# Where group 3's k is scaled: VectorE behind its q, or GpSimd behind the w_in loads

## The chip, the cores and the metric

The kernel runs on one core of a Trainium2 chip. The metric is the device time in microseconds (us). A core has five engines with instruction queues of their own: TensorE (PE in the profile, with its weight loads as PEld), VectorE (DVE), ScalarE (ACT), GpSimd (POOL) and SyncE (SP, which here only issues DMAs). Each engine runs its queue in order; engines wait for each other through semaphores.

## The reference

Attention with normalised q and k for 8 batches and 12 heads (448 rows, 64 columns each), then a feed-forward block whose input is the attention's output with the heads side by side:

```python
q_n = q / sqrt(mean(q * q, -1) + 1e-6) * g_q          # k_n in the same way, with g_k
scores = q_n @ k_n.T / 8
attn = softmax(scores)
x = (attn @ v), heads side by side                    # 3584 x 768
h = x @ w_in                                          # 768 x 2048
g = max(h, 0) + alpha * min(h, 0)
out = g @ w_out                                       # 2048 x 768, float32
```

## The kernel before

The 96 heads are worked on in 24 groups of four heads, three groups to a batch. A group's q and k go through the same steps:

- load_qk(y) issues the loads of q and k on SP, in natural order (128 partitions x 896 numbers each, float32). Four buffers named nat take turns; groups 2, 5 and 8 use places in a large tile called arena instead. A buffer is loaded again once the scale step of its former group has read it: q of group 6 goes where q of group 3 was, k of group 6 where k of group 3 was.
- square (line 376, on POOL) squares them, reduce (line 395, DVE) sums each row, and root (lines 416 and 417, ACT) makes the reciprocal root, rr.
- scale(y, q) and scale(y, k) (line 436) multiply by rr and write fp16. Groups 1, 3 and 5 write to places in the arena, one for q and one for k, so group 3 writes over group 1; other groups write to tiles named qs. The engine of this multiply is chosen in the code.
- turn(y) (lines 560 to 569) turns both with seven PE transposes each (q first) into two PSUM banks and copies them out on DVE into qT and kT. From group 9 on another layout without PE transposes is used (line 423 is its scale).
- score, soft: PE makes scores (line 588) and ACT takes the exponential (line 602), for each of 7 blocks j. den (PE, line 613), log and invert (ACT, lines 666 and 671) make the reciprocal sums; attend (PE, line 613) multiplies by v; times (DVE, line 709) scales the result into xT. Two groups of a batch share one den, log, invert and attend, "0+1"; the third has its own.

The feed-forward block follows batch by batch: begin and up (PE, line 726) multiply xT by w_in, slope (ACT, line 766) and larger (DVE, line 772) make g, and down and its successors multiply by w_out. begin(0) to begin(3) do the first two thirds of a product, those of groups 0 and 1, before group 2's xT is there; up(0,0) is the first that needs times(2,0,0).

The weights come through DMAs that POOL issues: load_w_in(c) has four issues of line 339 for each quarter c, and four more of line 347 where c is 0 or 2; load_w_out (line 353) and load_v (line 329) are issued there too. The issues of w_in wait for earlier ones to land when too many are under way. spin steps are PE work with no use but to keep PE busy.

follow(y, nm) (line 507) is a copy on POOL of one column of a scaled tile into a tile called mark; it makes POOL's queue follow what DVE wrote.

The order of all this is written out by hand: PLAN is a string of steps, read from front to back, and each step puts its instructions at the end of the queues of the engines that it uses. A step's place in the string thus sets its place in each queue, and nothing else. Around the change the string has root(3), invert(0+1), scale(3,q), score(2,2,0), load_w_in(3), two soft steps, two times steps, scale(3,k), square(4,q), times(0+1,0,0), turn(3).

Of the kernel before, what the change touches and what calls it, by code (L numbers as in the profile page):

```python
# [35 lines left out]
soft(1,2) score(0,5,1) score(1,1,0) soft(0,5) soft(1,1) score(1,5,0) turn(2) soft(1,5) score(1,6,1)  # L36
soft(1,6) reduce(3,q,None) score(1,4,0) score(2,0,0) soft(1,4) den(0+1,0) follow(1,k) soft(2,0)
log(0+1) load_qk(5) score(2,1,0) spin(1) reduce(3,k,0+1) attend(0+1,1,0) score(2,6,0) score(2,4,1)
attend(0+1,0,1) soft(2,1) root(3) score(2,3,1) invert(0+1) scale(3,q) score(2,2,0) load_w_in(3)
soft(2,4) soft(2,6) times(0+1,1,0) times(0+1,1,1) scale(3,k) square(4,q) times(0+1,0,0) turn(3)  # L40
score(2,5,0) square(4,k) load_qk(6) reduce(4,q,None) soft(2,3) soft(2,2) soft(2,5) den(2,0) log(2)
reduce(4,k,None) invert(2) attend(2,0,1) score(3,0,1) square(5,q) square(5,k) times(2,0,0)
score(3,1,0) begin(0) reduce(5,q) square(6,q) soft(3,0) begin(1) up(0,0,0) load_w_out(0) reduce(5,k)
# [150 lines left out]
def kernel(  # L194
# [12 lines left out]
    nc = tc.nc  # L207
# [7 lines left out]
    G = HH // 2  # L215
# [119 lines left out]
    def load_w_in(c):  # L335

        src = moe_w_in[:512].rearrange("(n x p) f -> n p x f", n=4, p=32)
        for n in range(4):
            nc.gpsimd.dma_start(
                out=w_in_sb[ds(32 * n, 32), :4, ts(c, FB)], in_=src[n, :, :, ts(c, FB)]  # L340
            )
        if c % 2 == 0:
            w = ts(c // 2, 2 * FB)
            src = moe_w_in[512:].rearrange("(n g e p) f -> e n p g f", n=2, g=2, e=2)
            for e in range(2):
                for n in range(2):
                    nc.gpsimd.dma_start(
                        out=w_in_sb[ds(64 * e + 32 * n, 32), 4:, w], in_=src[e, n, :, :, w]
                    )
# [11 lines left out]
    def square(y, nm):  # L361
        if y >= TD:
            t = nat[y, nm]
            sqs[y, nm] = t[:, :, HD:]
            nc.gpsimd.tensor_mul(out=sqs[y, nm], in0=t[:, :, :HD], in1=t[:, :, :HD])  # L365
            return
        src = nat[y, nm].rearrange("p h j d -> p (h j d)")
        sqf = sqs[y, nm].rearrange("p n d -> p (n d)")
        if (y, nm) == (1, "q"):
            nc.scalar.activation(out=sqf, in_=src, func=AF.Square)  # L370
        else:

            n = 2 if (y, nm) in ((2, "q"), (G, "k")) else 1
            for h in range(n):
                c = ts(h, 2 * J * D // n)
                nc.gpsimd.tensor_mul(out=sqf[:, c], in0=src[:, c], in1=src[:, c])
# [31 lines left out]
    def root(y, nms="qk"):  # L408
        n = len(nms)
        at = "qk".index(nms[0])  # L410
        if at == 0:
            rr_t[y] = ld.tile([128, 2, 2, 2, J], FP32, name="rr", tag="rr", bufs=2)
            if y < TD:
                rr_t[y] = rr_t[y][:, 0]
        rr, ss = rr_t[y][:, ds(at, n)], ss_t[y][:, ds(at, n)]
        nc.scalar.activation(out=rr, in_=ss, func=AF.Ln, scale=1.0 / D, bias=RMS_EPS)
        nc.scalar.activation(out=rr, in_=rr, func=AF.Exp, scale=-0.5)  # L417

    def scale(y, nm):
        if y >= TD:  # L420
            t = ld.tile([128, J, HD, 4], FP16, name="qs", tag="qs", bufs=3)
            r = rr_t[y][:, "qk".index(nm)].rearrange("p g h j -> p (g h) j")
            nc.gpsimd.tensor_mul(  # L423
                out=t.rearrange("p j d n -> p n j d"),
                in0=nat[y, nm][:, :, :HD].rearrange("p (n j) d -> p n j d", j=J),
                in1=r.unsqueeze(3).broadcast_to((128, 4, J, HD)),
            )
            qs[y, nm] = t.rearrange("p j d n -> p (j d n)").bitcast(FP32)
            return
        if y in (1, 3, 5):  # L430
            t = lent(HB + 4 * NB4 + "qk".index(nm) * NB4 // 2, NB4 // 2).bitcast(FP16)
            t = t.rearrange("p (j h d) -> p j h d", j=J, h=2)
        else:
            t = ld.tile([128, J, 2, D], FP16, name="qs", tag="qs", bufs=3)
        eng = nc.vector if y < G or (y, nm) == (G, "q") else nc.gpsimd
        eng.tensor_mul(
            out=t.rearrange("p j h d -> p h j d"),
            in0=nat[y, nm],
            in1=rr_t[y][:, "qk".index(nm)].unsqueeze(3).broadcast_to((128, 2, J, D)),
        )  # L440
        qs[y, nm] = t
# [101 lines left out]
    def turn(y):  # L543

        if y >= TD:
            for nm in "qk":
                if (y, nm) not in qkT:
                    flip(y, nm)
            return
        if y <= G or y > 2 * G:  # L550
            ps = [psf.tile([128, 512], FP32, name="tps", tag="mm") for _ in "qk"]
        else:
            ps2 = psa.tile([128, 2, 512], FP32, name="tps2", tag="acc")
            ps = [ps2[:, 0], ps2[:, 1]]
        tps = [
            t[:, : S].bitcast(FP16).rearrange("p (j c) -> p j c", j=J) for t in ps
        ]
        for tp, nm in zip(tps, "qk"):
            for j in range(J):
                nc.tensor.transpose(  # L560
                    tp[:, j, :], qs[y, nm][:, j].rearrange("p h d -> p (h d)"), ident
                )
        for tp, nm in zip(tps, "qk"):
            t = att.tile([128, J, 2, 64], FP16, name=f"{nm}T", tag=f"{nm}T", bufs=2)
            o = t.rearrange("p j g c -> p j (g c)")
            if nm == "q":
                nc.vector.tensor_copy(out=o, in_=tp)
            else:
                nc.vector.tensor_scalar(
                    out=o, in0=tp, scalar1=gain[:, 0:1], scalar2=None, op0=ALU.mult  # L570
                )
            qkT[y, nm] = t
# [7 lines left out]
    def score(y, j, spare=False):  # L580
        qT, kT = qkT[y, "q"], qkT[y, "k"]
        pool, tag = (psa, "acc") if spare else (pss, "sc")
        sc = pool.tile([128, 2, 512], FP32, name="sc", tag=tag)
        m = 64 if y < EARLY else 32
        for c in range(64 // m):
            for par in range(2):
                for g in range(2):
                    nc.tensor.matmul(  # L588
                        out=sc[ds(64 * g + m * c, m), par, :S].rearrange(
                            "p (j c) -> p j c", j=J  # L590
                        ),
                        lhsT=kT[ds(64 * par, 64), j, g, ts(c, m)],
                        rhs=qT[ds(64 * par, 64), :, g, :],
                        start=True,
                        stop=True,
                    )
        scs[y, j] = sc

    def soft(y, j):
        if j == 0:  # L600
            expT[y] = att.tile([128, J, 2, S], FP16, name="expT", tag="expT", bufs=EB)
        nc.scalar.activation(  # L602
            out=expT[y][:, j], in_=scs[y, j][:, :, :S], func=AF.Exp,
            scale=QK_SCALE, bias=EXP_BIAS,
        )
# [63 lines left out]
    def invert(ys):  # L669
        r = rden[ys]  # L670
        nc.scalar.activation(out=r, in_=r, func=AF.Exp, scale=-1.0)  # L671
# [3 lines left out]
    def attend(ys, half, spare=False):  # L675

        b, i = divmod(ys[0], G)
        v2 = vt[b].rearrange("p h j (e d) -> p h j e d", e=2)

        def weights(g, y, par, c, j):  # L680
            h = 2 * (y - G * b) + par
            return v2[ds(64 * g, 64), h, j, half if len(ys) == 2 else c]

        if half:
            av, accs = None, [psf.tile([128, 512], FP32, name="avb", tag="mm") for _ in range(2)]
        else:
            pool, tag = (pss, "sc") if spare else (psa, "acc")
            av = pool.tile([128, 2, 512], FP32, name="av", tag=tag)
            accs = (av[:, 0], av[:, 1])
        over_keys(accs, ys, weights)  # L690
        accum[ys, half] = av, accs

    def times(ys, half, k):
        b, i = divmod(ys[0], G)
        if b not in xT:
            xT[b] = att.tile([128, 2, G, S], FP16, name="xT", tag="xT")
        x, r = xT[b][:, :, i + half, :], rden[ys]
        av, accs = accum[ys, half]
        if half:
            o, p, q = x[:, k], accs[k][:, :S], r[:, k]  # L700
        elif halved(ys):
            n, e = divmod(k, 2)
            c = ts(n, S // 2)
            o, p, q = (
                x[ds(64 * e, 64), :, c], av[ds(64 * e, 64), :, c], r[ds(64 * n, 64)]
            )
        else:
            o, p, q = x, av[:, :, :S], r
        nc.vector.tensor_mul(out=o, in0=p, in1=q)  # L709
# [318 lines left out]
    def gains():  # L1028
# [6 lines left out]
        attend=attend, begin=begin, den=den, den_pre=den_pre, down=down, down_end=down_end,  # L1035
# [62 lines left out]
```

## Time and profile before

| | us |
|---|---|
| median of 3 runs (lowest, highest) | 414.73 (414.51, 415.57) |
| the profiled execution, its own time | 417.26 |
| its span in the profile | 415.05 |
| PE busy | 398.7 |
| DVE, ACT, POOL busy | 267.9, 270.1, 301.8 |
| mean granted PE clock | 0.986 |

The span reaches from the first to the last instruction of the program; its own time has some 2.2 us around that. All times below are from the span's start. A line of the profile gives an operation by engine, line in the code, what it writes and what it reads, and its shape (partitions x elements). The text in brackets at the end of a timeline line is the idle time of the engine just before it and what ended it. The granted clock is 1.00 at full speed and 0.50 at half.

### The profile page before, as it was taken

What the parts mean: (1) busy time and instruction counts of PE and PEld (TensorE: products, weight loads), DVE (VectorE), ACT (ScalarE), POOL (GpSimd) and SP (SyncE); (2) the same over time, 40 slices, a digit from 0 to 9 for tenths busy, and PEclk for the clock granted to TensorE, in tenths of its full rate; (3) what the DMA queues carried; (4) which work ended last, traced back from release to release, by engine and by line L of the source; (5) the groups of instructions that cost most, each with busy time, mean ns of one, the idle gap of its engine ahead of it and who ended that gap; (6) DMA issues with size and microseconds to landing.
All of it is one profiled execution on the core that took longest, in us unless ns stands there. A gap on an engine that the chain in (4) does not pass through costs nothing.

```text
span 415.1 us, 11991 instructions
## 1 busy us (share of the span) xinstructions
PE 398.7 (96%) x5083; PEld 211.3 (51%) x5083; DVE 267.9 (65%) x479; ACT 270.1 (65%) x405; POOL 301.8 (73%) x201
## 2 busy tenths in 40 slices
PE   7686999999999999999999999999999999999996
PEld 3333445554455554565455445545555455655664
DVE  3954777466766777678867858886668544654422
ACT  5585588657785786666897787876875885235110
POOL 6976999387978699998696996498597709700780
PEclk9988899999999999999999999999999999999999
DMA  7999499697877494849881695793707100230143
GB/s 267 209 261 207 79 246 202 110 244 174 172 141 191 126 229 80 200 99 216 198 187 45 168 203 151 159 212 83 191 21 133 32 2 23 58 77 0 30 102 100
DMA packets 37222, 58.40 MB, mean 141 GB/s; under 512 B 4768, under 2 KB 28976, under 8 KB 37168
## 3 DMA queue, kind: packets, MB, share of 16 engines
q1 hardware_dynamic: 23232, 45.43, 43.0%
q0 software_dynamic: 13536, 11.81, 19.3%
q8 instruction: 40, 0.66, 0.7%
q10 hardware_dynamic: 400, 0.39, 0.3%
q14 instruction: 14, 0.11, 0.1%
HBM read 58.40 MB, written 11.01 MB: 167 GB/s over the span
## 4 chain that ended last, share of the span: by engine, by line
PE 88%; DMA 4%; DVE 4%; POOL 2%; issue 1%; POOLq 0%
PE hT L726 25%; PE hTa L726 9%; PE sc L588 8%; PE op L792 7%; PE qx L854 5%; PE av L613 5%; PE qz L854 4%; PE qc L854 4%; PE oq L854 3%; PE dn L613 3%; PE qxa L854 3%; PE avb L613 2%; DMA w_in_sb<-in_moe_w_in_dram 2%; PE oqm L854 2%; DMA arena<-in_g_k_dram 2%; PE qza L854 1%
## 5 line engine op out<-in xcount | busy, mean ns | idle before, releaser
L602 ACT ACTIVATE expT<-sc 128x896 f16<-128x896 f32 x168 | 146.2, 916 | 46.2 <-PE sc L588 44.4
L726 PE MATMUL hT<-xT,w_in_sb 128*128 128x448 f16 x558 | 115.7, 353 | 0.3 <-DVE xT L709 0.2
L726 PEld LDWEIGHTS <-w_in_sb 128*128 128x128 f16 x768 | 73.0, 98 | 73.1 <-issue 8.8
L423 POOL TENSOR_TENSOR qs<-nat,rr 128x896 f16<-128x896 f32 x30 | 65.6, 2218 | 26.8 <-ACT rr L417 23.3
L766 ACT ACTIVATE gT<-hT,cols 128x448 f16<-128x448 f32 x92 | 58.4, 635 | 39.8 <-PE hT L726 38.8
L772 DVE TENSOR_TENSOR gT<-hT,gT 128x448 f16<-128x448 f32 x93 | 57.4, 619 | 38.4 <-ACT gT L766 37.7
L365 POOL TENSOR_TENSOR nat<-nat 128x896 f32<-128x896 f32 x30 | 50.6, 1695 | 8.4 <-DMA nat<-in_q_dram 8.1
L588 PE MATMUL sc<-qT,kT 64*32 64x448 f16 (+1 forms) x1092 | 50.0, 358 | 4.0 <-DVE kT L495 1.5
L854 PEld LDWEIGHTS <-gT 128*128 128x128 f16 x352 | 33.4, 98 | 25.5 <-issue 4.1
L726 PE MATMUL hTa<-xT,w_in_sb 128*128 128x448 f16 x198 | 42.9, 353 | 0.0
L709 DVE TENSOR_TENSOR xT<-av,rden 64x448 f16<-64x448 f32 (+1 forms) x37 | 27.2, 736 | 13.1 <-ACT rden L671 4.6
L842 POOL TENSOR_TENSOR gs<-gT 128x1024 f16<-128x1024 f16 x4 | 8.5, 2124 | 36.7 <-DVE gT L772 36.7
L588 PEld LDWEIGHTS <-kT 64*32 64x32 f16 (+1 forms) x1092 | 16.8, 94 | 33.0 <-issue 23.5
L386 DVE TENSOR_REDUCE sp<-nat 128x28 f32<-128x896 f32 x30 | 32.1, 1070 | 2.0 <-POOL nat L365 2.0
L792 PE MATMUL op<-w_out_sb,gT 128*128 128x384 f16 x176 | 30.3, 326 | 0.2 <-DVE xT L709 0.2
L766 ACT ACTIVATE gT<-hTa,cols 128x448 f16<-128x448 f32 x33 | 21.0, 635 | 10.5 <-PE hTa L726 10.0
L772 DVE TENSOR_TENSOR gT<-hTa,gT 128x448 f16<-128x448 f32 x33 | 20.4, 618 | 10.6 <-ACT gT L766 10.2
L613 PEld LDWEIGHTS <-vt 64*32 64x32 f16 x1344 | 19.8, 94 | 12.9 <-issue 2.7
L792 PEld LDWEIGHTS <-gT 128*128 128x128 f16 x192 | 18.3, 98 | 14.5 <-issue 3.0
L613 PE MATMUL av<-expT,vt 64*32 64x448 f16 x896 | 24.7, 354 | 0.0
L850 POOL TENSOR_TENSOR gT<-gT 128x1024 f16<-128x1024 f16 x11 | 23.5, 2133 | 0.0
L854 PEld LDWEIGHTS <-arena 128*128 128x128 f16 x136 | 12.6, 98 | 10.5 <-issue 2.6
(152 smaller groups left out, 576.9 us busy)
## 6 DMA issues: line engine op xcount, KB each, us to landing
nat<-in_q_dram SPq DMA_DIRECT2D x60, 216.0 KB, 4.2
nat<-in_k_dram SPq DMA_DIRECT2D x60, 216.0 KB, 5.0
out_dram<-osb SPq DMA_DIRECT2D x107, 96.0 KB, 3.4
vt<-in_v_dram POOLq DMA_DIRECT2D x8, 672.0 KB, 8.6
w_in_sb<-in_moe_w_in_dram POOLq DMA_DIRECT2D x24, 128.0 KB, 8.5
w_out_sb<-in_moe_w_out_dram POOLq DMA_DIRECT2D x4, 768.0 KB, 7.6
nat<-in_k_dram SPq DMA_DIRECT2D x6, 448.0 KB, 6.7
nat<-in_q_dram SPq DMA_DIRECT2D x5, 448.0 KB, 6.7
```

What stands on the lines that cost most here:

```text
L365: nc.gpsimd.tensor_mul(out=sqs[y, nm], in0=t[:, :, :HD], in1=t[:, :, :HD])
L386: nc.vector.tensor_reduce(out=parts[y][:, ts("qk".index(nm), 4 * J), :1], in_=sqs[y, nm], axis=AXIS_X, op=ALU.add,)
L423: nc.gpsimd.tensor_mul(out=t.rearrange("p j d n -> p n j d"), in0=nat[y, nm][:, :, :HD].rearrange("p (n j) d -> p n j d", j=J), in1=r.unsq ...
L588: nc.tensor.matmul(out=sc[ds(64 * g + m * c, m), par, :S].rearrange("p (j c) -> p j c", j=J), lhsT=kT[ds(64 * par, 64), j, g, ts(c, m)], r ...
L602: nc.scalar.activation(out=expT[y][:, j], in_=scs[y, j][:, :, :S], func=AF.Exp, scale=QK_SCALE, bias=EXP_BIAS,)
L613: nc.tensor.matmul(out=accs[g][ds(32 * n, 32), :S], lhsT=weights(g, y, par, c, j), rhs=expT[y][ds(64 * g, 64), j, par, :], start=(j == 0), ...
L709: nc.vector.tensor_mul(out=o, in0=p, in1=q)
L726: nc.tensor.matmul(out=hT[:, :S], lhsT=w_in_sb[:, block_of(g, i), ts(ft, 128)], rhs=xT[b][:, g, i, :], start=(i == 0 and g == 0), stop=(i ...
L766: nc.scalar.activation(out=g, in_=hT[:, :S], func=AF.Copy, scale=alpha_sb[:, ft : ft + 1])
L772: nc.vector.tensor_max(out=g, in0=hT[:, :S], in1=g)
L792: nc.tensor.matmul(out=op[:, :OH], lhsT=gT[:, ft, ts(tile % J, 128)], rhs=w_out_sb[:, ft, ts(oh, OH)], start=(ft == 0), stop=(ft == NF - 1),)
L854: nc.tensor.matmul(out=bank[:, c], lhsT=g[:, ft], rhs=v[:, ft, c], start=(first and ft == 0), stop=(ft == HF - 1), skip_group_check=True,)
```

## The change

Group 3's k is scaled on DVE instead of POOL, and the step moves in the plan from behind the times steps, where it also stood behind load_w_in(3), to right behind scale(3,q). For POOL nothing else changes its order; on DVE the multiply now stands ahead of the two times(0+1,1) steps.

```diff
-attend(0+1,0,1) soft(2,1) root(3) score(2,3,1) invert(0+1) scale(3,q) score(2,2,0) load_w_in(3)
-soft(2,4) soft(2,6) times(0+1,1,0) times(0+1,1,1) scale(3,k) square(4,q) times(0+1,0,0) turn(3)
+attend(0+1,0,1) soft(2,1) root(3) score(2,3,1) invert(0+1) scale(3,q) scale(3,k) score(2,2,0)
+load_w_in(3) soft(2,4) soft(2,6) times(0+1,1,0) times(0+1,1,1) square(4,q) times(0+1,0,0) turn(3)
...
-        eng = nc.vector if y < G or (y, nm) == (G, "q") else nc.gpsimd
+        eng = nc.vector if y <= G else nc.gpsimd
         eng.tensor_mul(
             out=t.rearrange("p j h d -> p h j d"),
             in0=nat[y, nm],
```

G is 3.

## The prediction

> **What bounds the kernel now.** I read the page first, then the chain of work in order of time, then the waits between 26 and 60 us, then the timeline of single engines around the moved step, and last the TensorE busy time cut at the edges where the granted clock changes. The page says that TensorE (PE) is the bound as a whole:
>
> ```profile
> PE 398.7 (96%) x5083; PEld 211.3 (51%) x5083; DVE 267.9 (65%) x479; ACT 270.1 (65%) x405; POOL 301.8 (73%) x201
> ```
>
> So PE is idle for only 415.05 - 398.7 = 16.4 us, and a change that is no PE work can gain only out of those, or out of time in which PE works at a lower clock. The chain in order of time (start, length, what) shows that the moved step stands in one of these holes:
>
> ```profile
> 28.07 8.70 DMA w_in_sb<-in_moe_w_in_dram
> ...
> 38.14 1.71 POOL arena L436
> ...
> 39.90 0.93 PE tps L560 x7
> ...
> 46.30 2.38 PE hT L726 x12
> 48.67 2.27 PE hTb L726 x12
> ```
>
> Up to 39.9 us the end is set by loads of w_in and then by GpSimd's (POOL's) one multiply of line 436, which is scale(3,k); from 39.9 us on the chain is PE work almost throughout. The waits (engine and line, who was waited for, total us, times, longest) name the hole and why the multiply is late:
>
> ```profile
> PE tps L560 <- POOL arena L436: 3.8, 1, 3.8
> POOL w_in_sb L339 <- DMA w_in_sb<-in_moe_w_in_dram: 2.6, 3, 1.1
> ```
>
> PE stands 3.8 us before the seven transposes of group 3's k. In POOL's timeline (start, length, engine, line, what) the multiply stands behind the four issues of load_w_in(3), each of which waits for an earlier w_in load to land:
>
> ```profile
> 32.71 0.64 POOL L507 COPY mark<-arena 128x1 f16<-128x1 f16 x1
> ...
> 37.05 1.07 POOL L339 DMA_DIRECT2D w_in_sb<-in_moe_w_in_dram  x2 [0.96 <-DMA w_in_sb<-in_moe_w_in_dram]
> 38.14 1.70 POOL L436 TENSOR_TENSOR arena<-nat,rr 128x896 f16<-128x896 f32 x1
> 39.79 3.31 POOL L376 TENSOR_TENSOR nat<-nat 128x896 f32<-128x896 f32 x2
> ```
>
> VectorE (DVE) has its own half of the pair, scale(3,q), done at 33.30, and what stands behind it is:
>
> ```profile
> 32.21 1.09 DVE L436 TENSOR_TENSOR arena<-nat,rr 128x896 f16<-128x896 f32 x1 [2.79 <-ACT rr L417]
> 33.22 1.15 DVE L709 TENSOR_TENSOR xT<-avb,rden 128x448 f16<-128x448 f32 x2
> 34.90 1.09 DVE L709 TENSOR_TENSOR xT<-av,rden 128x896 f16<-128x896 f32 x1 [0.53 <-PE av L613]
> ...
> 43.14 1.09 DVE L395 TENSOR_REDUCE ss<-nat 128x14 f32<-128x896 f32 x1 [0.55 <-POOL nat L376]
> 46.15 1.09 DVE L709 TENSOR_TENSOR xT<-av,rden 128x896 f16<-128x896 f32 x1 [1.92 <-PE sc L588]
> ```
>
> Last the stretches of 3.41 us (stretch, its length, PE busy, instructions, granted clock, DMA share, GB/s):
>
> ```profile
> 14.02:17.43 3.41, 2.11 (x18) 1.00 1.09 179
> 17.43:20.84 3.41, 1.81 (x26) 1.00 1.13 207
> 20.84:24.26 3.42, 3.39 (x18) 0.50 1.09 241
> ...
> 34.50:37.91 3.41, 1.52 (x31) 1.00 1.11 229
> 37.91:41.32 3.41, 1.42 (x19) 0.50 1.24 196
> 41.32:44.74 3.42, 3.42 (x84) 0.50 0.64 152
> 44.74:48.15 3.41, 3.41 (x67) 1.00 0.05 18
> ```
>
> The hole costs twice: a stretch with 1.52 or 1.42 us busy, and an earlier one with 1.81, is followed by a stretch at half clock; one with 2.11 is not. PE ran at half clock from 37.91 to 44.74, and it had work for all of it from 39.90 on.
>
> **The change, part by part.** *Removed from POOL:* one multiply, 1.70 us (38.14 row). POOL has no idle time between 37.05 and 52.4, so squares and scales behind it come 1.66 us earlier (39.79 becomes 38.13). The w_in(3) issues stay where they are; landings pace them.
>
> *Added to DVE:* one multiply of the same shape. The three rows of this line from natural order into the arena are 1.076, 1.091 and 1.398 us; I take 1.09, the row beside it, with 1.40 as the upper bound. It starts behind scale(3,q) at 33.30. One new wait: it writes the place where group 1's k lay, and the mark copy of follow(1,k) on POOL reads that place until 32.71 + 0.64 = 33.35. So it runs from about 33.4 to 34.5 and the wait costs 0.05 to 0.1. Queued behind it on DVE are the two halves of times(0+1,1) (to 35.6), times(0+1,0,0) (to 36.7), the copies of group 3's q and k, and the reductions of group 4. PE waits for these: the two halves free the two banks that the transposes of turn(3) use, and PE comes to those at 35.52, so nothing is late; times(0+1,0,0) frees the bank of score(2,5), which PE would reach at 36.4 and now gets at 36.75.
>
> *Moved on SP:* the step issues no DMA, but its end releases the load of group 6's k. This load is issued at 39.87 now and at about 34.5 then, while q of group 6 (issued 33.37, landed 9.8 us later) and the w_in loads are under way. Bounds: nothing, if it stands behind that q on SP's queue; up to 0.9 us, if from 34.5 to 37.05 three streams share what two shared (a third of 2.6 us), for the last w_in(3) issue. Below nothing is not possible for POOL, as more traffic cannot hurry those landings. I take nothing, since the q took 9.8 us on that queue; at worst its landing at 43.2 slips to that of the k, 45.8, 1.2 us past the new start of the square that reads it.
>
> *PE from 35.52:* 14 transposes to 36.4 (14 take 0.94 in the row at 54.79), score(2,5) at 36.75, soft(2,5) on ACT 0.92, den(2) 56 matmuls 1.45 us (chain at 77.24, at full clock) to 38.5, attend(2) 1.47 to 40.0, two scores 0.50 to 40.5, begin(0) and begin(1) 8 matmuls of 0.19 to 42.0. The next, up(0,0), needs times(2,0,0). ACT has log and invert of group 2 done at 40.5 (0.92 and 0.95 from 38.55), but on DVE times(2,0,0) is queued behind the reduction of group 4's k, which needs POOL's second square. **This is what is late next:** squares 38.13 to 41.43, reduction 1.09 to 42.57, times(2,0,0) 1.09 to 43.7, up(0,0) at 43.75. Now up(0,0) starts at 46.23 + 8 x 0.19 = 47.75. Difference 4.0 us, and PE has a new hole of 1.75 us.
>
> *How much of the 4.0 is clock.* At full clock throughout, PE would now need from 39.90: transposes 0.48, score 0.25, den 1.55 with its wait for soft(2,5), attend 1.45, scores 0.50, begins 1.52: up(0,0) at 45.6. So 2.15 us are clock loss in this execution and 1.85 are order of work. Nothing ties the edges of the stretches to an instruction; shifted over all positions, a hole of 3.82 us with a limit of about 1.95 busy costs 1.0 to 2.7 us, 1.75 in the mean. The new hole of 1.75 leaves at least 1.66 busy in a stretch. It falls under 1.81 busy for 57% of the positions and under 2.11 for 75%; I take 65%. The stretch behind it then costs half of 3.41, 1.7 us, since PE is full there: 1.1 in the mean. By the row, the new hole thus gives back over a quarter of the gain.
>
> The Trainium skill, "TensorE: Matmul & The Clock Gate", section "What's actually happening", says the clock falls to half after at least one idle window of about 3.4 us, and that the windows run freely. A hole of 1.75 us would by that rule cost no clock; the row at 17.43, 1.81 us busy and then half clock, is against it.
>
> *Behind that.* Everything in the PE order from up(0,0) on comes earlier together. The next POOL step that PE needs is scale(4,k), now ended at 52.39, then 50.74; turn(4)'s k transposes, at about 55.1 now, come at 51.1 with the full 4.0: just covered. larger(0,0) frees a bank for up(0,4): reduction of group 5's k at 45.85 on DVE, larger to 46.47, PE at 46.8: covered. scale(5,k) ends at 59.1 for transposes at 66.2, scale(6,k) at 70.8 for 76.3: 5 us and more of cover. From 84 us POOL has idle time (7.85 us before its scale) and PE is busy 99.8% from 200 to 300 us, so the lead is kept to the end.
>
> *The sum.* Mean: 1.85 + 1.75 - 1.1 = 2.5 us less. The profiled execution took 417.26 (span 415.05 and 2.2 around it); its own sum is 417.26 - 4.0 = 413.3 without and 415.0 with a half-clock stretch. The median of the runs, 414.73, lies 2.5 below it, of which its unlucky clock position explains some 0.4; I carry the mean difference over: 414.73 - 2.5 = **412.2 us**.
>
> **The rivals.**
> - *The new hole costs no clock.* For it: the 62% busy stretch at 14.02 kept its clock, and the new hole is half a stretch. Against: 53% did not. Time: 414.73 - 1.85 - 1.75 = 411.1. This is also the time by the rule of the Trainium skill above.
> - *POOL takes the lead away.* The earlier k load delays w_in(3) by 0.9 or q's landing by 1.2, or scale(4,k) becomes PE's next wait. For it: POOL is full from 37 to 52 and cover at turn(4) is only 0.3 at the full lead. Against: at a lead of 2.5 the cover is 1.8. Time: 1.2 less gain, 413.4.
> - *The change does not do what it says:* k is ready, but PE stands at the same place, as one of the banks or score(2,5) is late on DVE, now 1.1 us behind. Against: the wait list names POOL alone, 3.8 us. Time: 414.7.
> - *Slower: DVE waits behind POOL's mark.* The new wait ties DVE to POOL's queue, where the mark stands behind the last issue of load_w_in(2), which waits for a landing (32.18 now). Each us that the mark ends after 33.3 delays all DVE work named above. Up to 1.75 us are covered by the new hole; from 4.2 on the kernel is slower, from 5.5 measurably. Six give 414.73 - 2.5 + 4.25 = 416.5. Against: the mark ends at 33.35, and a late landing delays POOL now too.
>
> **How the numbers follow.** Within 0.3% is 1.24 us, about what a measurement can tell from no change. Hand-over to the squares with a half-clock stretch in some executions: 0.60, 411.3 to 413.3, centre 412.2. No clock loss: 0.17, 411.1. POOL takes the lead: 0.11, 413.4. No effect: 0.06. Slower: 0.06. The first three lie under 413.49 but for half of the third: faster 0.81, same 0.13, slower 0.06. The range goes from 410.6 (411.1 and the half us that runs scatter) to 413.9 (half of the third case and its scatter), leaving the last two out.
>
> **What would show it.** In the profile after: line 436 on DVE at 33.4 for 1.1 us, POOL's squares of group 4 at 38.1, the k transposes by 36.5; no wait of PE for POOL's arena, in its place one before an hT matmul for DVE xT, some 1.7 us at 42; DVE's reduction of group 4's k still ended by POOL; full clock at 38 to 44, perhaps half clock once after; k of group 6 issued at 34.5. I am wrong if the mark ends after 35, if the w_in(3) issues slip past 38.5, if turn(4) waits for POOL's qs, or if a lead at 60 us is gone at 200.

## The result and the profile after

| | before | after |
|---|---|---|
| median (lowest to highest) | 415.01 us (414.08 to 417.0, 6 runs) | 411.13 us (410.69 to 412.64, 6 runs) |
| ratio after to before, 95% interval | | 0.9894 (0.9863 to 0.9926) |
| profiled execution: own time, span | 417.26, 415.05 | 410.69, 408.62 |

The changed kernel is 1.1% faster, 3.9 us where 2.5 were forecast; the median lies within the range, and it is the time of the first rival (411.1: the new hole costs no clock). All ratios here leave out executions more than 1.5% above the fastest of their kernel, two of e5 and one of e12. The chain of work after the change, in order of time (start, length, what):

```profile
26.48 7.31 DMA w_in_sb<-in_moe_w_in_dram
...
35.24 0.07 POOL w_in_sb L339
...
35.80 3.34 POOL nat L376 x2
...
40.16 1.09 DVE xT L709
...
41.30 0.92 PE hT L726 x4
42.21 2.27 PE hTb L726 x12
```

The multiply of line 436 is no longer on it. Behind the last w_in(3) issue come POOL's two squares, then (with a reduction of 1.09 us that the chain shows as issue) times(2,0,0), then up(0,0): the new path of the prediction. DVE's timeline (start, length, engine, line, what, idle time before and its end):

```profile
29.90 1.09 DVE L436 TENSOR_TENSOR arena<-nat,rr 128x896 f16<-128x896 f32 x1 [2.79 <-ACT rr L417]
31.52 1.09 DVE L436 TENSOR_TENSOR arena<-nat,rr 128x896 f16<-128x896 f32 x1 [0.54 <-POOL mark L507]
32.53 1.15 DVE L709 TENSOR_TENSOR xT<-avb,rden 128x448 f16<-128x448 f32 x2
...
39.16 1.09 DVE L395 TENSOR_REDUCE ss<-nat 128x14 f32<-128x896 f32 x1 [0.55 <-POOL nat L376]
40.16 1.08 DVE L709 TENSOR_TENSOR xT<-av,rden 128x896 f16<-128x896 f32 x1
```

The multiply takes 1.09 us on DVE and waits for POOL's mark, as foreseen. On PE the 3.8 us wait for POOL's arena is gone, and one of 1.23 us stands ahead of up(0,0):

```profile
33.20 1.08 PE L560 MATMUL tps<-ident,arena 128*128 128x128 f16 x14
34.65 0.38 PE L588 MATMUL sc<-qT,kT 64*64 64x448 f16 x4 [0.36 <-ACT expT L602]
...
38.37 1.69 PE L726 MATMUL hT<-xT,w_in_sb 128*128 128x448 f16 x8
41.30 0.92 PE L726 MATMUL hT<-xT,w_in_sb 128*128 128x448 f16 x4 [1.23 <-DVE xT L709]
```

The clock stays full there (stretch, length, PE busy, instructions, granted clock, DMA share, GB/s):

```profile
34.20:37.61 3.41, 3.05 (x118) 1.00 1.08 296
37.61:41.02 3.41, 2.45 (x32) 1.00 0.91 170
41.02:44.44 3.42, 3.15 (x17) 1.00 0.07 13
```

The two spans differ by 6.4 us, more than the medians. A part is the opening, which the change does not touch: scale(3,q) starts at 32.21 in the profile before and at 29.90 in this one. Over all fourteen profiles of this study its start lies between 29.90 and 32.21, and the last w_in(3) issue, where its place in the plan is the old one, follows 3.1 to 7.4 us behind it, as the loads land. I therefore read distances inside an execution:

| profile | last w_in(3) issue, from scale(3,q) | up(0,0), from scale(3,q) | up(0,0) behind that issue | at half clock ahead of up(0,0) | up(0,0) to the end |
|---|---|---|---|---|---|
| before | 5.37 | 15.54 | 10.17 | 6.83 | 367.30 |
| before again (e8) | 3.54 | 13.09 | 9.55 | 3.41 | 367.29 |
| before, hole filled (e3) | 5.03 | 13.10 | 8.07 | none | 368.03 |
| after | 5.34 | 11.40 | 6.06 | none | 367.33 |
| the plan's edit alone (e1) | 7.17 | 13.22 | 6.05 | none | 367.32 |
| the engine's edit alone (e2) | 4.64 | 10.69 | 6.05 | none | 367.45 |
| after again (e12) | 7.37 | 13.42 | 6.06 | none | 368.95 |

(From the starts in the timelines; up(0,0) is the ninth hT matmul. The half clock is that between scale(3,q) and up(0,0).) The last column says that what is won at up(0,0) is kept to the end, but for 0.7 us in e3 and 1.6 in e12 (both below). The fourth says where it is won: 8.07 - 6.06 = 2.0 us are order, and 10.17 - 8.07 = 2.1 or 9.55 - 8.07 = 1.5 are clock.

### The profile page after: what moved, and what is told of

Its sections match the earlier page's. It is cut to its first block, busy times and chain, and to the rows that moved or that the text cites. A ratio compares the mean times of both kernels' runs of the same rounds, so it can differ in the third digit from the quotient of the medians.

```text
span 408.6 us, 11992 instructions
## 1 busy us (share of the span) xinstructions
PE 395.3 (97%) x5083; PEld 210.3 (51%) x5083; DVE 268.3 (66%) x480; ACT 270.4 (66%) x405; POOL 299.9 (73%) x200
## 4 chain that ended last, share of the span: by engine, by line
PE 88%; DVE 4%; DMA 3%; POOL 3%; issue 1%; POOLq 0%; DVEq 0%
PE hT L726 25%; PE hTa L726 9%; PE sc L588 8%; PE op L792 7%; PE qx L854 5%; PE av L613 5%; PE qz L854 4%; PE qc L854 4%; PE oq L854 4%; PE qxa L854 3%; PE avb L613 2%; PE dn L613 2%; PE oqm L854 2%; DMA w_in_sb<-in_moe_w_in_dram 2%; POOL nat L376 2%; DMA arena<-in_g_k_dram 2%
```

## Experiments

**e1: the plan's edit alone.** The changed plan with the old choice of engine.

```diff
-        eng = nc.vector if y <= G else nc.gpsimd
+        eng = nc.vector if y < G or (y, nm) == (G, "q") else nc.gpsimd
```

> The plan's edit alone: k of group 3 is scaled by POOL, but ahead of the w_in(3) issues. Theory (the order counts: k has to be out from behind the paced issues, the engine is nearly free): POOL does the multiply in about 33.4 to 35.1 in the clock of the profile before, inside idle time in which it waits for landings, the last w_in(3) issue keeps its time, the squares of group 4 start where they start in the changed kernel. 411.1 +- 0.5, as the changed kernel. Rival (it is VectorE's faster multiply, or POOL's 1.7 us less work, that brings the gain): the squares come 1.7 us later than in the changed kernel, 412.9 to 415.0.

Measured: 412.67 us (410.09 to 415.44, 10 runs), ratio to before 0.994 (0.9906 to 0.9974). POOL's timeline:

```profile
33.47 0.20 POOL L507 COPY mark<-arena 128x1 f16<-128x1 f16 x1
33.75 1.68 POOL L436 TENSOR_TENSOR arena<-nat,rr 128x896 f16<-128x896 f32 x1
35.38 0.60 POOL L339 DMA_DIRECT2D w_in_sb<-in_moe_w_in_dram  x1
36.31 1.19 POOL L339 DMA_DIRECT2D w_in_sb<-in_moe_w_in_dram  x2 [0.33 <-DMA w_in_sb<-in_moe_w_in_dram]
38.16 0.54 POOL L339 DMA_DIRECT2D w_in_sb<-in_moe_w_in_dram  x1 [0.66 <-DMA w_in_sb<-in_moe_w_in_dram]
38.71 3.32 POOL L376 TENSOR_TENSOR nat<-nat 128x896 f32<-128x896 f32 x2
```

The multiply runs in time in which POOL would have waited; the last issue still waits 0.66 us for a landing, so the multiply did not delay it. up(0,0) is 6.05 us behind that issue, as after. The landings were late in this execution (7.17 us). The median lies above the 411.1 +- 0.5 of the theory and just below the 412.9 to 415.0 of the rival, and the interval of the ratio, 411.2 to 414.0 us, reaches into both, so the time decides nothing. The distance does: the order counts.

**e2: the engine's edit alone.** The plan of before, with DVE as the engine, so the multiply stands behind the two times(0+1,1) steps.

```diff
-        eng = nc.vector if y < G or (y, nm) == (G, "q") else nc.gpsimd
+        eng = nc.vector if y <= G else nc.gpsimd
```

> The engine's edit alone: VectorE scales k in the old place of the plan, behind the two times(0+1,1) steps. Theory: the multiply runs on VectorE some 1.2 us later than in the changed kernel, times(0+1,0,0) is as late as there, the transposes of k move by less than 0.5 us, and the new hole of PE covers that: 411.1 +- 0.5. Rival (the place behind q counts): later by the 1.2 us, 412.3.

Measured: 412.31 us (410.79 to 416.16, 10 runs), ratio 0.9926 (0.9894 to 0.9958); up(0,0) 6.05 us behind the last w_in(3) issue. The median is the time of the rival, 412.3, and not the 411.1 +- 0.5 of the theory. But the rival's mechanism, a later k that PE has to wait for, is not in the profile: the multiply runs behind the two times(0+1,1) steps and ahead of times(0+1,0,0), and PE goes through the 14 transposes without a wait for DVE.

```profile
32.44 1.08 DVE L436 TENSOR_TENSOR arena<-nat,rr 128x896 f16<-128x896 f32 x1
```

The changed kernel itself was measured at 412.54 us when it was run again (e12), so the 411.1 that both forecasts started from was low. Either edit alone moves k out from behind the paced issues, and either alone gives the full distance. The times cannot tell the two from each other or from the changed kernel.

**e3: before, with its hole filled.** 16 matmuls without use into the bank that the k transposes then overwrite.

```diff
-        for tp, nm in zip(tps, "qk"):
+        for n, (tp, nm) in enumerate(zip(tps, "qk")):
+            if (y, nm) == (G, "k"):
+                for _ in range(16):
+                    nc.tensor.matmul(
+                        out=ps[n][:, :S], lhsT=ident, rhs=idle, start=True, stop=True
+                    )
             for j in range(J):
                 nc.tensor.transpose(
```

> The kernel before with 16 matmuls without use (128 rows, 448 columns, 0.19 us each, 3.0 us together) between group 3's q and k transposes, where PE stands 3.8 us. Order, waits and results are those of the kernel before; only PE is busy in the hole. Theory (part of the gain is the clock that the hole costs): full clock from 38 to 45, k transposes at the same time, up(0,0) earlier by the clock loss, 1.75 in the mean: 415.0 - 1.75 = 413.3, and in the profile up(0,0) some 13.4 us behind the start of scale(3,q) instead of 15.5. Rival (the clock does not matter, the whole 3.9 us are order): 415.0 or up to 0.5 later.

Measured: 414.18 us (412.91 to 416.99, 12 runs) beside 415.1 (35 runs), ratio 0.9973 (0.9944 to 1.0003). It lies between the 413.3 of the theory and the 415.0 of the rival, and the time alone is not clear of no change. The timeline of PE and the stretches:

```profile
34.37 3.19 PE L561 MATMUL tps<-gT,ident 128*128 128x448 f16 x16
38.01 0.56 PE L565 MATMUL tps<-ident,arena 128*128 128x128 f16 x7 [0.45 <-POOL arena L436]
...
38.82 1.66 PE L618 MATMUL dn<-expT,ones 64*32 64x448 f16 x56
```

```profile
33.04:36.45 3.41, 3.34 (x42) 1.00 1.11 254
36.45:39.86 3.41, 2.96 (x57) 1.00 1.18 196
39.86:43.28 3.42, 3.42 (x94) 1.00 0.38 132
```

PE still waits for POOL's multiply, at the same distance from the w_in(3) issues, but den(2) takes 1.66 us where it took 2.82 before, and up(0,0) starts 13.10 us behind scale(3,q), 13.4 forecast. The mean granted clock agrees: 0.990 in the median of before's 35 executions beside it, 0.996 in that of the 12 of this kernel. A stretch of 3.41 us at half clock is worth 0.004 of the span, so before has one or two such stretches more. So the clock loss of the old hole was real, 1.5 to 2.1 us at up(0,0). In this profile 0.7 us of it is lost again (last column of the table) at 77 us: 56 matmuls of attend take 2.27 us there, where they take 1.52 at 80.59 in before, and in their midst PE waits for nothing that the profile shows.

```profile
77.93 0.95 PE L618 MATMUL avb<-expT,vt 64*32 64x448 f16 x31 [0.40 <-issue]
```

Why it stands there stays open. If it does so in the other executions too, 0.8 to 1.4 us are left of the clock's part; the medians differ by 0.9.

**e4: after, with its hole filled.** Six such matmuls ahead of up(0,0).

```diff
-begin(1) up(0,0,0)
+begin(1) fill(6) up(0,0,0)
```

(fill is a new step, six such matmuls into a tile of its own; its code is left out here.)

> The changed kernel with 6 such matmuls (1.14 us) ahead of up(0,0), in the new hole of PE before xT of group 2. If the new hole costs clock in most executions, as in my sum (1.1 in the mean): 411.1 - 1.1 = 410.0. If it costs none (the rival in the prediction, for which the measured 411.1 speaks): 411.1 +- 0.3, and the granted clock stays full in both.

Measured: 412.51 us (411.73 to 414.25, 12 runs), ratio 0.9936 (0.9909 to 0.9963). A miss: neither forecast. In its profile the landings were early, the last w_in(3) issue only 4.05 us behind scale(3,q), and xT was ready when PE came to it. There was no hole to fill, and the filler delayed up(0,0):

```profile
40.09 1.69 PE L726 MATMUL hT<-xT,w_in_sb 128*128 128x448 f16 x8
41.61 1.30 PE L999 MATMUL fill<-gT,ident 128*128 128x448 f16 x6
```

The new hole thus has no fixed size: the landings set POOL's side of it, and PE's side lies some 10 us behind scale(3,q) (10.01 in e6, 10.03 in e11, 10.35 in e9).

**e5: load_w_in(3) behind group 4's squares**, so that POOL squares in the time in which it waits for landings.

```diff
-load_w_in(3) soft(2,4) ... times(0+1,1,1) square(4,q) times(0+1,0,0) turn(3)
-score(2,5,0) square(4,k) load_qk(6)
+soft(2,4) ... times(0+1,1,1) square(4,q) times(0+1,0,0) turn(3)
+score(2,5,0) square(4,k) load_w_in(3) load_qk(6)
```

> The changed kernel with load_w_in(3) behind group 4's two squares in the plan. Theory (the new path is landings of w_in, POOL's last w_in(3) issue, two squares, reduction, times(2,0,0), up(0,0)): POOL squares in the time in which it now waits for landings, some 2 to 3 us earlier, the issues then wait for nothing; up(0,0) is bound by PE itself, the new hole of 1.2 to 1.75 us closes, and scale(4,k) comes some 2 us earlier, so that turn(4) keeps its cover: 411.1 - 1.2 to 1.75 = 409.4 to 409.9. Rival (the later w_in(3) loads or a later wait take it back): 411.1 or more.

Measured: 414.2 us (411.24 to 419.67, 12 runs), ratio 0.9956 (0.9927 to 0.9985): the gain is mostly gone. POOL, then DVE:

```profile
30.75 0.71 POOL L507 COPY mark<-arena 128x1 f16<-128x1 f16 x1
31.42 3.31 POOL L376 TENSOR_TENSOR nat<-nat 128x896 f32<-128x896 f32 x2
34.69 2.21 POOL L339 DMA_DIRECT2D w_in_sb<-in_moe_w_in_dram  x4
```

```profile
30.33 5.36 DVE L436 TENSOR_TENSOR arena<-nat,rr 128x896 f16<-128x896 f32 x2 [2.79 <-ACT rr L417]
35.61 1.14 DVE L709 TENSOR_TENSOR xT<-avb,rden 128x448 f16<-128x448 f32 x2
```

POOL did what was forecast, but the k multiply on DVE took 4.20 of the 5.36 us: it began beside POOL's squares and ended 0.96 us after they had ended at 34.73. The times steps behind it were late by this, and PE stood for them ahead of turn(3):

```profile
36.28 1.50 PE L560 MATMUL tps<-ident,arena 128*128 128x128 f16 x14 [2.58 <-DVE xT L709]
```

3.41 us at half clock followed (36.48 to 39.90), and up(0,0) came 13.49 us behind scale(3,q). That is a mechanism that neither theory had.

**e6: times(2,0,0) ahead of the reduction of group 4's k.**

```diff
-reduce(4,k,None) invert(2) attend(2,0,1) score(3,0,1) square(5,q) square(5,k) times(2,0,0)
+invert(2) attend(2,0,1) times(2,0,0) reduce(4,k,None) score(3,0,1) square(5,q) square(5,k)
```

> The changed kernel with times(2,0,0) ahead of the reduction of group 4's k on VectorE. Theory: up(0,0) is then bound by PE, the new hole closes, but POOL is as late as before, and PE next stands at turn(4) for scale(4,k), of which the cover is 0.3 to 0.4 us: gain 0.3 to 0.4 only, 410.7, with a wait of PE for POOL's qs of about 0.8 us in the profile. Rival (POOL is no bound there): 409.4 to 409.9.

Measured: 411.91 us (410.21 to 414.15, 8 runs), ratio 0.9931 (0.9902 to 0.996): inconclusive in time. In the profile landings were early (3.76 us) and there would have been little hole; up(0,0) starts 10.01 us behind scale(3,q), which is PE's own limit. PE shows no wait for POOL's qs, but one of 0.24 us for larger(0,0), and 0.4 us more from up(0,0) to the end than after.

**e7: the mark late**, the mechanism of the slower rival.

```diff
-soft(1,4) den(0+1,0) follow(1,k) soft(2,0)
+soft(1,4) den(0+1,0) load_w_in(3) follow(1,k) soft(2,0)
```

(and load_w_in(3) taken out behind score(2,2,0))

> The changed kernel with load_w_in(3) ahead of follow(1,k), so that POOL's mark stands behind four more paced issues, and VectorE's multiply waits for the mark: the mechanism of the slower rival, with the mark about 4.5 us later. By the rival's price (each us beyond the 1.75 that the new hole covers costs one): 411.1 + 2.7 = 413.8, with up to 2 more where PE's hole then costs clock: 413.8 to 415.8. In the profile, VectorE idle some 5 us before line 436, ended by the mark. If VectorE does not wait for the mark, 411.1.

Measured: 423.2 us (422.7 to 423.88, 4 runs), ratio 1.0187 (1.0153 to 1.0221). DVE waits for the mark, then the multiply itself takes 9.08 us. POOL, then DVE:

```profile
35.82 0.20 POOL L507 COPY mark<-arena 128x1 f16<-128x1 f16 x1
35.96 3.31 POOL L376 TENSOR_TENSOR nat<-nat 128x896 f32<-128x896 f32 x2
39.24 3.31 POOL L376 TENSOR_TENSOR arena<-arena 128x896 f32<-128x896 f32 x2
42.51 1.67 POOL L376 TENSOR_TENSOR nat<-nat 128x896 f32<-128x896 f32 x1
44.13 0.95 POOL L353 DMA_DIRECT2D w_out_sb<-in_moe_w_out_dram  x1
```

```profile
36.05 9.08 DVE L436 TENSOR_TENSOR arena<-nat,rr 128x896 f16<-128x896 f32 x1 [3.55 <-POOL mark L507]
```

It ends at 45.13, 0.95 us after the last of five squares in a row (44.18), though those have nothing to do with its data. PE stood 10.94 us ahead of turn(3), had half clock for 13.65 us from 37.77 on, and came to up(0,0) 22.96 us behind scale(3,q). The rival's price was too low by this: 413.8 to 415.8 were forecast.

**e8: before again.** No edit.

> The kernel before itself, for the clock and the opening of its other executions. By the theory the mean granted clock is below 1 in all its executions (at least 3.4 us at half clock, 0.996 or less, behind the hole), and the place of scale(3,q) moves by a us or two from one execution to another. 415.0 +- 0.6.

Measured: 414.22 us (413.59 to 417.0, 10 runs), ratio to the other runs of before 1.0001 (0.9969 to 1.0033); so the median is a little below the forecast of 414.4 to 415.6, without a change that can be told. Mean clocks are 0.985 to 0.995, so all of them lose some; not all of that is the hole's, as the profile has a stretch at half clock in the opening, too (20.52 to 23.93). Its hole is only 1.98 us, as the landings came early, and it is still followed by 3.41 us at half clock (PE's timeline, then the stretches):

```profile
36.88 0.56 PE L560 MATMUL tps<-ident,arena 128*128 128x128 f16 x7 [1.98 <-POOL arena L436]
```

```profile
34.17:37.58 3.41, 1.43 (x22) 1.00 1.14 254
37.58:40.99 3.41, 3.41 (x76) 0.50 0.94 213
```

**e9: e5, with POOL held until DVE has scaled k.** One more step to e5's plan.

```diff
-times(0+1,1,1) square(4,q) times(0+1,0,0)
+times(0+1,1,1) follow(3,k) square(4,q) times(0+1,0,0)
```

> As e5 (load_w_in(3) behind group 4's two squares), and POOL copies one column of the scaled k into its mark ahead of the first square, so that it begins to square only when VectorE's multiply is done. Theory (in e5 and e7 the multiply stood still while POOL squared, 4.2 and 9.1 us instead of 1.1): the multiply takes 1.1 us again, the squares start 2.4 us behind the start of scale(3,q) whatever the landings are, up(0,0) is bound by PE, 10.2 us behind that start, where the changed kernel has 9.8 to 11.5 with the landings: 0.6 us less in the mean than the changed kernel run beside it, and 0 to 1.2 in one execution. Rival (the multiply was slow in e5 for another reason than POOL's squares beside it): it takes 4 us again and nothing is won.

Measured: 411.22 us (410.05 to 412.48, 6 runs), ratio 0.987 (0.984 to 0.9901). DVE, then POOL:

```profile
33.38 1.09 DVE L436 TENSOR_TENSOR arena<-nat,rr 128x896 f16<-128x896 f32 x1 [0.47 <-POOL mark L507]
...
35.46 1.08 DVE L709 TENSOR_TENSOR xT<-av,rden 128x896 f16<-128x896 f32 x1
```

```profile
34.53 0.19 POOL L507 COPY mark<-arena 128x1 f16<-128x1 f16 x1 [1.19 <-DVE arena L436]
34.68 3.31 POOL L376 TENSOR_TENSOR nat<-nat 128x896 f32<-128x896 f32 x2
37.94 2.20 POOL L339 DMA_DIRECT2D w_in_sb<-in_moe_w_in_dram  x4
```

With nothing else changed in the plan but that POOL waits for it, the multiply takes 1.09 us again: the squares beside it were the cause in e5. PE runs into up(0,0) without a hole, 10.35 us behind scale(3,q).

**e10: after, with square(4,q) done twice** (POOL's removed 1.7 us put back behind k).

```diff
-square(4,q) times(0+1,0,0)
+square(4,q) square(4,q) times(0+1,0,0)
```

> The changed kernel with square(4,q) done twice on POOL (same result): 1.66 us of POOL work put back where the change took its multiply away, but behind k. Theory (POOL's chain of w_in issues and squares sets up(0,0) now): from the last w_in(3) issue to up(0,0) 6.06 + 1.66 = 7.7 us, PE's hole before up(0,0) up to 2.9 us, 411.1 + 1.0 to 1.7 by the landings. If a hole of this kind costs clock as the old one did, 1.7 more in the executions where the record falls to half. Rival (POOL is not on the path behind the change): 411.1 +- 0.3.

Measured: 414.8 us (411.39 to 416.92, 10 runs), ratio 0.9959 (0.9927 to 0.9991); up(0,0) 7.82 us behind the last w_in(3) issue, 7.7 forecast:

```profile
42.18 0.92 PE L726 MATMUL hT<-xT,w_in_sb 128*128 128x448 f16 x4 [0.75 <-DVE xT L709]
```

POOL's chain sets up(0,0), and POOL work is on the path one for one where PE has to wait for it. The hole is small here, as the landings came early (3.13 us). The time is more than the forecast 412.1 to 412.8, and 2.3 us above the changed kernel beside it (e12), for 1.66 us of work; the granted clock does not explain that, since two executions of 415.42 and 415.99 us had a mean of 1.0. What does stays open.

**e11: e5 with POOL scaling k ahead of its squares.**

```diff
-        eng = nc.vector if y <= G else nc.gpsimd
+        eng = nc.vector if y < G or (y, nm) == (G, "q") else nc.gpsimd
```

> As e5, but POOL scales k itself, ahead of its squares (e1's order with load_w_in(3) behind the squares): no two-input multiply of VectorE beside POOL's squares at all, and no wait of POOL for VectorE. Theory: k is out some 3.4 us behind the start of scale(3,q), the squares run from 3.4 to 6.7, up(0,0) is bound by PE at 10.2 to 10.4 us: as e9, within 0.3. Rival (VectorE's slow multiply was not what made e5 lose): 2 us more than the changed kernel, as e5.

Measured: 411.55 us (410.75 to 413.47, 6 runs), ratio 0.9889 (0.9858 to 0.9921); up(0,0) 10.03 us behind scale(3,q), no hole. As e9.

**e12: after again**, beside e9 to e11.

> The changed kernel itself, beside e9 to e11 on the same chip and for more executions: 411.1 +- 0.5, up(0,0) 6.06 us behind the last w_in(3) issue or, where the landings come early, bound by PE at 10.2 us behind the start of scale(3,q).

Measured: 412.54 us (409.87 to 416.91, 9 runs), ratio 0.991 (0.9874 to 0.9945). The median misses its forecast of 410.6 to 411.6. The profile is the slowest execution, that of 416.91 us: the last w_in(3) issue came 7.37 us behind scale(3,q), up(0,0) again 6.06 behind that, the hole before it was 2.11 us, and half clock followed once (stretches as above):

```profile
42.03:45.44 3.41, 1.34 (x8) 1.00 0.31 51
45.44:48.85 3.41, 3.41 (x11) 0.50 0.15 10
```

So the new hole cost clock in this one execution, where the landings were late: from up(0,0) to the end it took 368.95 us, 1.6 more than after. In e1 a hole of 2.33 us cost none. e9 has the lowest median of the three kernels run beside it, 411.22 us, 1.3 below the 412.54 here (0.6 forecast), and no hole that depends on landings; the intervals of the two ratios overlap, so that it beats the changed kernel is likely, not shown.

## Why the prediction was right, and where it was off

- *POOL's 1.70 us and the order:* right. The squares start 0.56 us behind the last w_in(3) issue, up(0,0) 6.06 behind it in after, e1, e2 and e12. Order was worth 2.0 us (e3 against after), 1.85 forecast; e10 puts the POOL work back and up(0,0) comes 1.76 us later behind the issue. Where the landings are early, PE itself is the bound and order should be worth less: with those of e8 it is 3.54 + 8.07 - 10.0 = 1.6 us by these distances, an estimate. Not each of the four w_in(3) issues waits for a landing, as the prediction has it: its wait row counts three.
- *The old hole's clock:* right. 2.1 us in the first profile, 1.5 in e8 (2.15 and a mean of 1.75 forecast), and filling the hole takes it away (e3).
- *DVE's multiply and its wait:* right in time and place, 1.09 us. It started 1.62 us behind scale(3,q), not 1.1 to 1.2, as the mark came 0.5 us later; PE's new hole covered that, as it was to. score(2,5) waited 0.36 us, about as forecast, but the profile names ACT's exponential for it and not times(0+1,0,0). The bound of 1.40 us was no bound: 4.20 and 9.08 us were measured in e5 and e7. The row of 1.398 us that I took it from already showed the cause, since POOL squared until 17.08 us beside it and it ended 0.95 us later, and so did the mark of 0.64 us at 32.71 in the profile before, against 0.20 after: it ended at 33.35, with DVE's multiply.
- *The k load on SP:* nothing seen against it. It is issued at 32.64, q of group 6 ahead of it (31.05), and the last w_in(3) issue comes 5.34 us behind scale(3,q), 5.37 before. As that distance runs from 3.1 to 7.4 us between executions, a delay of some tenths by the earlier load is not excluded; no run changes the load alone.
- *What is late next:* right. PE waits for DVE's xT behind POOL's squares; turn(4) shows no wait, with scale(4,k) ended at 48.41 and its transposes from some 48.8 on.
- *The new hole's clock, the step that failed:* 1.1 us were taken off the gain, a stretch of 1.7 us at odds of 65%. The term goes back to a hole of 1.75 us in every execution. It is 1.23 in after, 0.5 in e2, nothing in e4's execution and 2.1 to 2.3 where landings are late, since one side of it hangs on them; e1's 2.33 us even kept full clock. In after the least busy stretch has 2.45 of 3.41 us. Where it did strike, in e12, it cost 1.6 us, so the size of a strike was right; what was too high is how often it was taken to strike. The mean clocks of the runs show no sign of it: their median is 0.996 over the 15 executions of the changed kernel and 0.9945 over the 12 of e9 and e11, whose profiles have no such hole; 1.1 us would be 0.003. With no clock in it, the sum is 2.0 + 1.5 to 2.1 = 3.5 to 4.1 us, and 3.9 were measured. e12, with 415.75 - 412.54 = 3.2, lies between that and the forecast of 2.5, so whether the mean cost is nothing or some tenths stays open. The first rival, at 0.17, should have had more.
- *The median carried over from one profile:* the positions of the landings and the opening spread single executions by 3 us and more (before from 412.21 to 417.7 in 35 runs), which I had put down to the clock's position alone.

## What to carry to other kernels

A small step that stands in one queue behind issues paced by landings is as late as those landings; either another engine or another place in the same queue frees it, and the gain is cut by whatever then comes behind the same issues. A multiply on VectorE with both inputs in SBUF must be looked at together with what GpSimd runs at that moment: here it was free only because GpSimd was waiting. Where executions differ by more than the effect, measure distances between two fixed instructions within each profile.

## What was not expected of the hardware

*VectorE and GpSimd in each other's way.* The DVE multiply reads two SBUF tiles. Beside POOL's squares it took 4.20 us (e5) and 9.08 us (e7), ending 0.96 and 0.95 us after the last square; with POOL waiting it took 1.09 (after, e9). Other DVE work beside squares kept its length: times(0+1,0,0), with one of its two inputs in PSUM, took 1.08 us at 35.46 in e9, and the reduction at 43.14 in before, with one input, took 1.09. The Trainium skill, "SBUF — State Buffer", section "Who interferes with whom", says that a VectorE instruction with two SBUF inputs contends with a GpSimd instruction that reads SBUF, and that the later one to issue blocks fully. The runs agree, and show that squares in a row do not let it in between them.

*The clock after part-idle stretches.* In the first 58 us of the fourteen profiles 20 stretches of 3.41 us at full clock were at most 57% busy on PE; 17 were followed by half clock, and 3 were not (44% in e1, 55% in e2 and e11). None that was busier was (the next has 57.5%). So the limit read from two rows, 53 and 62%, holds mostly, but not always, and what tells the three apart stays open; e1's is this one, followed by full clock:

```profile
40.36:43.77 3.41, 1.51 (x8) 1.00 0.57 100
43.77:47.19 3.42, 2.98 (x16) 1.00 0.02 3
```

The Trainium skill, "TensorE: Matmul & The Clock Gate", section "What's actually happening", ties half clock to at least one idle window of about 3.4 us; here stretches that were half busy were enough.
